# A spectral and gated kernel on one core: eight token tiles instead of six by the seven-product scheme in the first chunk, and GpSimd's stores as operations of the scheduler

## The chip, the cores and the metric

The kernel runs on one core of a Trainium2 chip. The metric is device time in microseconds (us) of one execution; lower is better. Matrix products run on TensorE (PE in the profile, its weight loads PEld), elementwise work on VectorE (DVE) and ScalarE (ACT); GpSimd (POOL) only issues DMA stores and SyncE (SP) only DMA loads. A matmul reads a 128x128 and a 128x512 operand from the on-chip memory and adds up in one of eight PSUM banks.

## The reference

For a sequence of 2048 tokens of 512 features in fp32, it computes the sum of the input, a Fourier mixing and a gated feed-forward of the layer-normed input:

```python
xn = _layernorm(x, axis=-1)
return x + _A_ref(xn, ...) + _B_ref(xn, ...)
# _A_ref: a = xn @ Wre.T; b = xn @ Wim.T      (hidden DFT, 512 x 512)
#         y = Cre @ a - Cim @ b               (sequence DFT, 2048 x 2048)
# _B_ref: h = gelu(xn @ w_gate) * (xn @ w_up); out = h @ w_down   (512 -> 1792 -> 512)
```

## The kernel before

**The products.** Every fp32 operand is split into a high part (rounded, by ScalarE: `split_hi`, L240) and a low part (operand minus high part, by VectorE: `split_lo`, L243). `mm3` (L254) makes a product from three matmuls (high with high, low with high, high with low), all recorded at L257. So a panel loaded from memory passes ScalarE, then VectorE, then TensorE. In the profile `psh`/`psl` and `z311h`/`z311l` are such pairs of parts.

**The sequence DFT** is made in four chunks of 512 output columns, c = 0 to 3. Its token tiles are taken in pairs (k, k+8). A pair's part of a chunk is a 2 by 2 block product. It is made in one of two ways:

- *plain* (only in chunk 0): two panels for each tile and four blocks of columns, 24 matmuls a tile, results in the `z` banks;
- by *seven products* (a Strassen-Winograd form): sums of the DFT blocks and of the tokens are made on VectorE, and seven products are taken in two steps (p = 0: r = 0, 5, 6, 4 with 24 matmuls; p = 1: r = 1, 3, 2 with 18), 42 a pair, in the `m` banks. Step p = 0 loads three panels, makes three sums (`sum_step`, L614) and parks the third, t2, in memory with a GpSimd store; step p = 1 loads t2 again. At the end of a chunk's p = 0 steps ScalarE and VectorE empty the banks (`after`, L1421: the rows L1426 to L1436), and the p = 1 products use the same banks again.

`J` (L31) lists the pairs that go by seven products in chunk 0. From c = 1 on all eight pairs do.

**The hidden DFT.** From the results of chunk 0 and 1, the products y with numbers r = 0, 1 (after chunk 0) and r = 4, 2, 6, 5, 3 (after chunk 1) are made, each in two halves g of 12 matmuls. Their operands z are split like all others (`z400h` is r = 4, g = 0, first half, high part). Each y is copied by ScalarE into two `part` buffers (L542), which GpSimd stores to `partial` in memory: r = 0, 5, 6 plainly (L544 is that store's line, L546 the other's), r = 1, 2, 3, 4 adding to what stands there. One call, `y_out` (L539), makes copies and stores.

**What sets the order.** All operations of the chunks 0 and 1 and of the y products after them, with the first loads and splits of chunk 2, are handed to a list scheduler, `Plan` (L34), and from chunk 2 on the order is written by hand. An operation is added (`add`) with its engine, its cost in us, what must come before it, buffers that it makes and uses, a due time, and mb, the size of its DMA. `deadlines` (L66) works due times back from TensorE's order; an operation that empties a bank gets the end of its product plus 4 unless it is given one. `choose` (L104) takes the earliest that can begin, with more urgent ones preferred; `run` (L142) keeps the clocks. Buffers are 109 of one size (128x512), of which the plan uses 107; a buffer is free again when its last user has ended, and the engine that takes it next then waits for that user, for example for a store's landing. Of DMAs the plan knows a transfer time of 2.6 us per MB, and, for SP's loads only, that no more than eight may be in flight. GpSimd's stores stood inside other operations: the stores of y within the copies on ScalarE, the park of t2 within the third sum on VectorE, a store of `xd` within a subtraction; the plan's own operations on GpSimd's queue for these did nothing (`lambda: None`). The copies of the five last y sums carry a fixed due time:

```python
        plan.add(("yo", r), "a", 1.04, lambda r=r: y_out(0, r), after=[("y", r, 1), *OUT.get(r, ())], makes={("po", r): 2}, holds=both,
                 due=END + 54.4)
        plan.add(("yd", r), "g", 1.2, lambda: None, after=[("yo", r)], uses=[("po", r)], mb=2 * MB)
```

END is the plan's time for the end of chunk 1's products.

Of the kernel before, what the change touches and what calls it, by code (L numbers as in the profile page):

```python
# [11 lines left out]
AF = mybir.ActivationFunctionType  # L12
OP = mybir.AluOpType

P = 128
S = 2048
# [13 lines left out]
SLOTS = 109  # L30
J = (5, 6, 7)  # L31
NP = NF
# [3 lines left out]
class Plan:  # L36
# [15 lines left out]

    def add(self, name, engine, cost, fn, after=(), makes=(), uses=(), due=None, mb=0, banks=(), holds=()):
# [5 lines left out]
        self.ops[name] = dict(e=engine, cost=cost, fn=fn, after=after, makes=dict(makes), due=due, mb=mb, banks=tuple(banks), drains=bool(holds) and engine != "p")  # L59
        self.size.update(makes)  # L60
        for k in (*dict(makes), *uses):
            self.users.setdefault(k, set()).add(name)
        for k in (*banks, *holds):
            self.held.setdefault(k, set()).add(name)

    def deadlines(self):  # L66
# [27 lines left out]
        for n in order:  # L94
# [47 lines left out]
    def run(self):  # L142
# [25 lines left out]
        while any(ready.values()):  # L168
# [39 lines left out]
def fnet_geglu_kernel(ctx: ExitStack, tc: tile.TileContext, x, xt, cs, dh, wgu, wd, out):  # L208
# [299 lines left out]

    yps, zraw, zt = {}, {}, {}

# [12 lines left out]

    def sub_xd(sp, j):
        nc.vector.tensor_sub(xd[sp, j, 0], xd[sp, j, 0], xd[sp, j, 1])
        nc.gpsimd.dma_start(partial[sp, 2, j], xd[sp, j, 0])

    def y_block(r, g, b, js=range(2), first=True):
# [4 lines left out]
        for part in (slice(2), slice(2, 3)):  # L533
            for e in range(2):
                for j in js:
                    mm3(yps[r, j], [u[:, e] for u in dop[r, g]], cols(j), b[e], first and e == 0, not first and e == 1,
                        part=part, late=1)

    def y_out(sp, r, js=range(2)):  # L539
        for j in js:  # L540
            t = slot("part")
            nc.scalar.activation(t, yps[r, j], AF.Copy)  # L542
            if r in (0, 5, 6):
                nc.gpsimd.dma_start(partial[sp, r, j], t)  # L544
            else:
                nc.gpsimd.dma_start(partial[sp, r, j], t, accum_op=OP.add)  # L546

# [65 lines left out]

    def sum_step(i):  # L614

# [618 lines left out]
    plan.dma, land = 12.8, 8.75  # L1234
    plan.flying["s"] = [4.4, 5.7, 7., 8.1]
    for t in range(2, X_AHEAD):
        plan.done(("x", XO[t]), land)
        plan.flying["s"].append(land)
        land += .675
    for i in range(3, LOAD_AHEAD):  # L1240
        plan.done(("pan", i), land)
        plan.flying["s"].append(land)
        land += .675
# [144 lines left out]
    def step_ops(i, late=None):  # L1388
# [3 lines left out]
        def s(j):  # L1392
            if not box:
                box.extend(sum_step(i))
# [180 lines left out]
    for r, g in ((0, 0), (0, 1), (1, 0), (1, 1)):  # L1575
# [3 lines left out]
        if g:  # L1579
            plan.add(("yo", r), "a", 1.04, lambda r=r: y_out(0, r), after=[("y", r, g), *([("res", 0, 0)] if r else ["st2"])],  # L1580
                     makes={("po", r): 2}, holds=[("y", r, j) for j in range(2)])
            plan.add(("yd", r), "g", 1.2, lambda: None, after=[("yo", r)], uses=[("po", r)], mb=2 * MB)
        if (r, g) == (0, 0):
# [14 lines left out]
    for j in range(2):  # L1598
        plan.add(("xd", j), "s", .9, lambda j=j: load_xd(0, j), makes={("xd", j): 2}, mb=2 * MB)
        plan.add(("xds", j), "v", V5, lambda j=j: sub_xd(0, j), after=[("xd", j)], uses=[("xd", j)], due=END - 12)  # L1600
        plan.add(("xdp", j), "g", .01, lambda: None, after=[("xds", j)], uses=[("xd", j)], mb=MB, due=END - 8)
    for kb in range(2):
# [6 lines left out]
    for r in (4, 2, 6, 5, 3):  # L1609
        both = [("y", 1, r, j) for j in range(2)]  # L1610
        for g in range(2):
            plan.add(("y", r, g), "p", 12 * MM, lambda r=r, g=g: z_y(r, g), uses=[("do", r, g)] + [("z", (r, g, e)) for e in range(2)],
                     after=[("dlo", r, g), *(("zlo", (r, g, e)) for e in range(2))], banks=both * (g == 0), holds=both)
        plan.add(("yo", r), "a", 1.04, lambda r=r: y_out(0, r), after=[("y", r, 1), *OUT.get(r, ())], makes={("po", r): 2}, holds=both,
                 due=END + 54.4)
        plan.add(("yd", r), "g", 1.2, lambda: None, after=[("yo", r)], uses=[("po", r)], mb=2 * MB)
    END += 10 * 12 * MM
# [131 lines left out]
```

## Time and profile before

| | |
|---|---|
| time, three runs | 804.59 us median (804.32 to 807.07) |
| the profiled execution | 804.45 us, with a span of 802.4 us |
| TensorE | 794.4 us busy, 3493 instructions, clock granted in full |
| VectorE | 718.8 us busy, 1330 instructions |
| ScalarE | 504.9 us busy, 950 instructions |
| GpSimd | 156.4 us busy, 227 instructions |

The profile is of one execution. A busy TensorE says little alone, since matmuls overlap: what counts is their pitch, the time between the starts of two. Engines wait for each other by semaphores, and the trace names for each wait the engine or DMA that ended it, by inference. Chunk 0 takes the span up to about 90 us, chunk 1 from about 100 to 176 us, the y products between and behind them up to 205 us; the gated part begins near 390 us.

### The profile page before, as it was taken

Reading aid. Unit: us, or ns where it says so; the run is one execution under the profiler, and the core shown is the slowest. Engines: PE = TensorE matmul, PEld = TensorE weight load, DVE = VectorE, ACT = ScalarE, POOL = GpSimd, SP = SyncE. Lnnn points to the kernel's source line nnn. Section 1 sums busy time; section 2 is a strip of 40 time slices with the busy share of each in tenths; the row PEclk is TensorE's granted clock in tenths of the full one; section 3 lists DMA queues with packets and bytes.
Section 4 is the critical chain, followed back from the end, with each engine's and each line's share of the span. In section 5 each row is a group of like instructions: output and inputs, shape, how many; then the busy total and the mean of one; then the engine's idle time right before and its main releaser. Section 6 shows DMA issues by size and latency. Waiting matters only on the chain.

```text
span 802.4 us, 11459 instructions
## 1 busy us (share of the span) xinstructions
PE 794.4 (99%) x3493; PEld 654.4 (82%) x3493; DVE 718.8 (90%) x1330; ACT 504.9 (63%) x950; POOL 156.4 (19%) x227
## 2 busy tenths in 40 slices
PE   9999999999899999999999999999999999999998
PEld 6888888888688888888888888888888888888886
DVE  7999999969899979899999998898778779989787
ACT  6786566547444465364758776766766677576564
POOL 0001410034211131000203423321221233121100
PEclk9999999999999999999999999999999999999999
DMA  9737797868999988778825987868965799887842
GB/s 333 283 119 259 268 353 256 281 230 233 349 351 315 350 289 296 256 272 268 203 79 128 218 161 172 189 109 217 255 126 96 128 232 153 174 211 137 250 105 105
DMA packets 90110, 176.69 MB, mean 220 GB/s; under 512 B 10784, under 2 KB 14400, under 8 KB 89856
## 3 DMA queue, kind: packets, MB, share of 16 engines
q1 hardware_dynamic: 65040, 117.75, 43.7%
q0 software_dynamic: 24720, 57.95, 33.7%
q8 instruction: 27, 0.44, 0.2%
q14 instruction: 35, 0.29, 0.1%
q10 hardware_dynamic: 288, 0.26, 0.1%
HBM read 113.77 MB, written 65.29 MB: 223 GB/s over the span
## 4 chain that ended last, share of the span: by engine, by line
PE 97%; DMA 1%; DVE 1%; ACT 0%; issue 0%; SPq 0%; DVEq 0%; ACTq 0%
PE m L257 31%; PE dn L257 17%; PE b L257 14%; PE c L257 10%; PE a L257 9%; PE y L257 8%; PE z L257 7%; DMA pan<-in_cs 1%; PE warm L1191 1%; DVE psl L246 0%; ACT part L542 0%; DVE dl L246 0%; DVE zr L1514 0%; DVE z410l L246 0%; ACT dh L241 0%
## 5 line engine op out<-in xcount | busy, mean ns | idle before, releaser
L241 ACT ACTIVATE psh<-pan 128x512 fp32r<-128x512 f32 x189 | 108.7, 626 | 82.1 <-DVE pan L628 30.0
L246 DVE TENSOR_TENSOR psl<-pan,psh 128x512 fp32r<-128x512 f32 x189 | 121.3, 682 | 6.0 <-ACT psh L241 5.3
L907 POOL DMA_DIRECT2D partial<-part x94 | 80.9, 870 | 234.0 <-ACT part L906 200.7
L257 PE MATMUL m<-psl,xch 128*128 128x512 f32 x216 | 84.2, 390 | 0.1
L257 PE MATMUL m<-psh,xch 128*128 128x512 f32 x216 | 84.1, 390 | 0.0
L257 PE MATMUL m<-psh,xcl 128*128 128x512 f32 x216 | 84.1, 389 | 0.0
L906 ACT ACTIVATE part<-dn 128x512 f32<-128x512 f32 x94 | 55.4, 604 | 24.2 <-PE dn L257 22.4
L246 DVE TENSOR_TENSOR wl<-ws,wh 128x512 fp32r<-128x512 f32 x84 | 55.1, 684 | 0.1
L241 ACT ACTIVATE wh<-ws 128x512 fp32r<-128x512 f32 x84 | 49.7, 629 | 0.1
L257 PEld LDWEIGHTS m<-psl,xch 128*128 128x128 f32 x216 | 40.6, 188 | 9.1 <-DVE psl L246 0.6
L257 PEld LDWEIGHTS m<-psh,xch 128*128 128x128 f32 x216 | 40.6, 188 | 8.3
L257 PEld LDWEIGHTS m<-psh,xcl 128*128 128x128 f32 x216 | 40.6, 188 | 8.3
L1131 ACT ACTIVATE w<-b 128x512 f32<-128x512 f32 x28 | 16.7, 598 | 47.1 <-PE b L257 47.0
L624 POOL DMA_DIRECT2D t_park<-pan x27 | 15.1, 558 | 140.3 <-DVE pan L624 90.6
L1134 DVE TENSOR_TENSOR w<-c,w 128x512 f32<-128x512 f32 x28 | 19.3, 689 | 24.6 <-ACT w L1131 24.6
L246 DVE TENSOR_TENSOR htl<-s,hth 128x512 fp32r<-128x512 f32 x56 | 36.0, 686 | 4.5 <-ACT hth L241 4.4
L879 DVE TENSOR_TENSOR s<-s 128x512 f32<-128x512 f32 x56 | 37.4, 688 | 1.0
L257 PE MATMUL m<-psh,xa 128*128 128x512 f32 x108 | 37.7, 389 | 0.0
L623 DVE TENSOR_TENSOR pan<-pan 128x512 f32<-128x512 f32 x54 | 35.3, 678 | 0.0
L246 DVE TENSOR_TENSOR wl<-wx,wh 128x512 fp32r<-128x512 f32 x28 | 19.2, 686 | 16.3 <-ACT wh L241 16.3
L241 ACT ACTIVATE hth<-s 128x512 fp32r<-128x512 f32 x56 | 32.4, 642 | 1.0 <-DVE s L879 1.0
L241 ACT ACTIVATE hh<-s 128x512 fp32r<-128x512 f32 x42 | 26.7, 635 | 9.8 <-DVE s L866 7.3
(779 smaller groups left out, 2379.2 us busy)
## 6 DMA issues: line engine op xcount, KB each, us to landing
pan<-in_cs SPq DMA_DIRECT2D x155, 256.0 KB, 5.4
partial<-part POOLq DMA_DIRECT2D x122, 256.0 KB, 5.1
wx<-in_wgu SPq DMA_DIRECT2D x56, 256.0 KB, 4.9
wd<-in_wd SPq DMA_DIRECT2D x28, 256.0 KB, 4.3
acc<-partial SPq DMA_DIRECT2D x28, 256.0 KB, 5.6
t_park<-pan POOLq DMA_DIRECT2D x27, 256.0 KB, 4.8
pan<-t_park SPq DMA_DIRECT2D x27, 256.0 KB, 4.4
zr<-z_park SPq DMA_DIRECT2D x16, 256.0 KB, 4.9
```

The lines of the kernel that those rows point to most:

```text
L241: nc.scalar.activation(t[0], src, AF.Copy, scale=float(sign))
L246: engine.tensor_sub(t[1], src, hi)
L257: nc.tensor.matmul(ps, a[u][:, sl], b[v], start=first and r == 0, stop=last and r == 2, skip_group_check=resumed)
L623: return [lambda: nc.vector.tensor_sub(t3, b22, b12), lambda: nc.vector.tensor_sub(t1, b12, b11), lambda: (nc.vector.tensor_sub(b22, b22, ...
L624: lambda: (nc.vector.tensor_sub(b22, b22, t1), nc.gpsimd.dma_start(t2_park[c, k], b22))]
L879: nc.vector.tensor_sub(t, u, v)
L906: nc.scalar.activation(t, ps[j], AF.Copy)
L907: nc.gpsimd.dma_start(partial[sp, r, j], t, accum_op=OP.add)
L1131: nc.scalar.activation(w, b, AF.Copy)
L1134: nc.vector.tensor_add(w, c, w)
L1191: nc.tensor.matmul(ps, warm[:, :P], warm, start=i == 0, stop=False)
```

## The change

Four edits. `J` gets a fourth pair: chunk 0 has eight plain tiles instead of ten, and four pairs by seven products. GpSimd's stores of y, of t2 and of xd become operations of the scheduler on GpSimd's queue; t2's load then comes after the park's operation instead of after the sum. The scheduler counts transfers in flight on both queues (SP eight, GpSimd seven, an accumulating store as two) and takes an accumulating transfer as 3.3 times as long. The copies of the last five y sums lose their fixed due time.

```diff
-J = (5, 6, 7)
+J = (4, 5, 6, 7)
...
+    def parts(self, o):
+        return round(o["mb"] / .262) * (2 if o["adds"] else 1)
...
                 if e == "s":
-                    at = max([at, o["due"] - self.ahead] + self.flying[e][-8:][:1] * (len(self.flying[e]) > 7))
+                    at = max(at, o["due"] - self.ahead)
+                if o["mb"]:
+                    k, room = self.parts(o), 8 if e == "s" else 7
+                    for when, u in reversed(self.flying[e]):
+                        k += u
+                        if k > room:
+                            at = max(at, when)
+                            break
...
-                self.dma = max(self.dma, at + o["cost"] + 1.1) + o["mb"] * 2.6
+                self.dma = max(self.dma, at + o["cost"] + 1.1) + o["mb"] * 2.6 * (3.3 if o["adds"] else 1)
                 end = self.dma + self.LAND
-                self.flying[e].append(end)
+                self.flying[e].append((end, self.parts(o)))
...
+    def y_copy(r, js=range(2)):
+        for j in js:
+            ypart[r, j] = slot("part")
+            nc.scalar.activation(ypart[r, j], yps[r, j], AF.Copy)
+
+    def y_send(sp, r, js=range(2)):
+        for j in js:
+            nc.gpsimd.dma_start(partial[sp, r, j], ypart.pop((r, j)), **({} if r in (0, 5, 6) else {"accum_op": OP.add}))
...
-                    lambda: (nc.vector.tensor_sub(b22, b22, t1), nc.gpsimd.dma_start(t2_park[c, k], b22))]
+                    lambda: (nc.vector.tensor_sub(b22, b22, t1), park or nc.gpsimd.dma_start(t2_park[c, k], b22))]
...
-                     after=[("S", i - (HS - FIRST[c]), 2)] if key == "t2" else [])
+                     after=[("park", i - (HS - FIRST[c]))] if key == "t2" else [])
...
-            plan.add(("park", i), "g", .01, lambda: None, after=[("S", i, 2)], mb=MB, uses=[("r", i, b22)])
+            plan.add(("park", i), "g", .6, lambda: nc.gpsimd.dma_start(t2_park[c, k], pan_src[i][5]), after=[("S", i, 2)], mb=MB, uses=[("r", i, b22)])
...
-        plan.add(("yo", r), "a", 1.04, lambda r=r: y_out(0, r), after=[("y", r, 1), *OUT.get(r, ())], makes={("po", r): 2}, holds=both,
-                 due=END + 54.4)
-        plan.add(("yd", r), "g", 1.2, lambda: None, after=[("yo", r)], uses=[("po", r)], mb=2 * MB)
+        plan.add(("yo", r), "a", 1.04, lambda r=r: y_copy(r), after=[("y", r, 1), *OUT.get(r, ())], makes={("po", r): 2}, holds=both)
+        plan.add(("yd", r), "g", 1.2, lambda r=r: y_send(0, r), after=[("yo", r)], uses=[("po", r)], mb=2 * MB, adds=r in (1, 2, 3, 4))
```

The copies and sends of r = 0 and 1 and the stores of xd are changed in the same way. The changed kernel's line numbers are 10 to 16 higher (the products L267, high splits L251, low splits L256). It has 3474 matmuls of the products' helper in place of 3480. From chunk 2 on, every engine's order is the same in both kernels.

Three places show what the scheduler makes of it. First ScalarE after chunk 1, where the y products begin: `part` rows are copies of y sums, the first two those of r = 4 and the next two of r = 2; `dh` are high parts of the hidden DFT matrix, `z600h` and the like high parts of z. Before:

```order
L241 ACTIVATE z600h_2197<-zt_2119 128x512
L241 ACTIVATE z601h_2206<-zt_2201 128x512
L241 ACTIVATE dh_2211<-ds_2174 128x512
L241 ACTIVATE dh_2227<-ds_2209 128x512
L241 ACTIVATE dh_2232<-d_2074 128x512
L542 ACTIVATE part_2235<-y_2132 128x512
L542 ACTIVATE part_2238<-y_2133 128x512
L241 ACTIVATE z610h_2244<-zt_2230 128x512
```

And now:

```order
L251 ACTIVATE z600h_2213<-zt_2133 128x512
L553 ACTIVATE part_2216<-y_2146 128x512
L553 ACTIVATE part_2218<-y_2147 128x512
L251 ACTIVATE z601h_2224<-zt_2211 128x512
L251 ACTIVATE dh_2230<-ds_2227 128x512
L251 ACTIVATE dh_2249<-ds_2188 128x512
L251 ACTIVATE dh_2252<-d_2089 128x512
L251 ACTIVATE z610h_2257<-zt_2247 128x512
```

The copies of r = 4 stood behind z601h and three matrix splits and now stand directly behind z600h. Second ScalarE some fifteen rows later, at the end of the y products, with the semaphores that each row waits for (DMASW: a GpSimd transfer, DMAHW: an SP load). Before, the last z splits, the copies of r = 5 and the first panels of chunk 2 (`psh`):

```order
L241 ACTIVATE z301h_2347<-zr_2081 128x512 [waits DMASW5_49,DVE_49,Activation_49]
L241 ACTIVATE z310h_2363<-zr_2091 128x512 [waits DMASW7_49,DVE_49,Activation_49]
L241 ACTIVATE z311h_2377<-zr_2093 128x512 [waits DVE_49]
L542 ACTIVATE part_2401<-y_2314 128x512 [waits DMASW4_49,DMAHW0_49,DMASW2_49,PE_49]
L542 ACTIVATE part_2404<-y_2315 128x512 [waits PE_49,Activation_49]
L241 ACTIVATE psh_2412<-pan_2296 128x512 [waits DMAHW4_49]
L241 ACTIVATE psh_2415<-pan_2408 128x512 [waits DMASW1_49,DVE_49]
```

And now:

```order
L553 ACTIVATE part_2394<-y_2327 128x512 [waits PE_49,Activation_49]
L553 ACTIVATE part_2396<-y_2328 128x512 [waits DMASW3_49,PE_49]
L251 ACTIVATE psh_2408<-pan_2094 128x512 [waits DMAHW2_49,Activation_49]
L251 ACTIVATE psh_2411<-pan_2400 128x512 [waits DMASW4_49,DVE_49,Activation_49]
L251 ACTIVATE z310h_2420<-zr_2322 128x512 [waits DVE_49]
L251 ACTIVATE z311h_2423<-zr_2324 128x512 [waits DMASW5_49,DVE_49,Activation_49]
L251 ACTIVATE psh_2429<-pan_2401 128x512
```

Two panel splits and the copies now stand ahead of z310h and z311h, and psh_2411 and z311h take the buffers of the two r = 2 copies (the transfers DMASW4 and DMASW5 there); before, the buffer of the second r = 2 copy went to VectorE's row z311l. Third VectorE at the end of chunk 1's p = 0 steps, where the banks m are emptied (`c22` and `m4` are the last four of these adds; `pan` is a sum of panels and `psl` a panel's low part). Before:

```order
L1434 TENSOR_TENSOR c22_1794<-m4_1361,u2_1776 128x512
L1434 TENSOR_TENSOR c22_1800<-m4_1369,u2_1786 128x512
L1436 TENSOR_TENSOR m4_1361<-m4_1361,p0_1747 128x512
L1436 TENSOR_TENSOR m4_1369<-m4_1369,p0_1753 128x512
L246 TENSOR_TENSOR psl_1741<-pan_1533,psh_1740 128x512
```

And now:

```order
L1450 TENSOR_TENSOR c22_1785<-m4_1346,u2_1770 128x512
L644 TENSOR_TENSOR pan_1482<-pan_1466,pan_1482 128x512
L1450 TENSOR_TENSOR c22_1799<-m4_1353,u2_1777 128x512
L256 TENSOR_TENSOR psl_1758<-pan_1426,psh_1757 128x512
L1452 TENSOR_TENSOR m4_1346<-m4_1346,p0_1741 128x512
L1452 TENSOR_TENSOR m4_1353<-m4_1353,p0_1749 128x512
```

A panel sum and a low split now stand between the adds. Counted from the start, the first of these m4 adds is VectorE's 305th row before and its 304th now; at the same place of chunk 0 it is the 187th before and the 177th now.

More of the change, by code (lines that the diff above doesn't have):

```diff
@@ L51, in done, with add @@
         self.ends[name] = at
-    def add(self, name, engine, cost, fn, after=(), makes=(), uses=(), due=None, mb=0, banks=(), holds=()):
+    def add(self, name, engine, cost, fn, after=(), makes=(), uses=(), due=None, mb=0, banks=(), holds=(), adds=False):
         after = list(after)
@@ L58, in add @@
             self.products = name
-        self.ops[name] = dict(e=engine, cost=cost, fn=fn, after=after, makes=dict(makes), due=due, mb=mb, banks=tuple(banks), drains=bool(holds) and engine != "p")
+        self.ops[name] = dict(e=engine, cost=cost, fn=fn, after=after, makes=dict(makes), due=due, mb=mb, adds=adds, banks=tuple(banks), drains=bool(holds) and engine != "p")
         self.size.update(makes)
@@ L522, in load_xd, with sub_xd @@
             nc.sync.dma_start(xd[sp, j, h], xt[sp, 1, 2 * h + j])
-    def sub_xd(sp, j):
+    def sub_xd(sp, j, park=False):
         nc.vector.tensor_sub(xd[sp, j, 0], xd[sp, j, 0], xd[sp, j, 1])
-        nc.gpsimd.dma_start(partial[sp, 2, j], xd[sp, j, 0])
+        if not park:
+            nc.gpsimd.dma_start(partial[sp, 2, j], xd[sp, j, 0])
     def y_block(r, g, b, js=range(2), first=True):
@@ L537, in y_block @@
                         part=part, late=1)
+    def y_copy(r, js=range(2)):
[5 more added lines that the diff above has]
+            nc.gpsimd.dma_start(partial[sp, r, j], ypart.pop((r, j)), **({} if r in (0, 5, 6) else {"accum_op": OP.add}))
     def y_out(sp, r, js=range(2)):
         for j in js:
[L541 to L546, printed above, removed]
+            y_copy(r, [j])
+            y_send(sp, r, [j])
     def fetch_z(sp, kb, g):
@@ L1234, in fnet_geglu_kernel @@
     plan.dma, land = 12.8, 8.75
-    plan.flying["s"] = [4.4, 5.7, 7., 8.1]
+    plan.flying["s"] = [(t, 1) for t in (4.4, 5.7, 7., 8.1)]
     for t in range(2, X_AHEAD):
         plan.done(("x", XO[t]), land)
-        plan.flying["s"].append(land)
+        plan.flying["s"].append((land, 1))
         land += .675
@@ L1241, in fnet_geglu_kernel @@
         plan.done(("pan", i), land)
-        plan.flying["s"].append(land)
+        plan.flying["s"].append((land, 1))
         land += .675
@@ L1599, in fnet_geglu_kernel @@
         plan.add(("xd", j), "s", .9, lambda j=j: load_xd(0, j), makes={("xd", j): 2}, mb=2 * MB)
-        plan.add(("xds", j), "v", V5, lambda j=j: sub_xd(0, j), after=[("xd", j)], uses=[("xd", j)], due=END - 12)
-        plan.add(("xdp", j), "g", .01, lambda: None, after=[("xds", j)], uses=[("xd", j)], mb=MB, due=END - 8)
+        plan.add(("xds", j), "v", V5, lambda j=j: sub_xd(0, j, True), after=[("xd", j)], uses=[("xd", j)], due=END - 12)
+        plan.add(("xdp", j), "g", .6, lambda j=j: nc.gpsimd.dma_start(partial[0, 2, j], xd[0, j, 0]), after=[("xds", j)], uses=[("xd", j)], mb=MB, due=END - 8)
     for kb in range(2):
```

10 lines of the change are left out of this document (5 added, 5 removed).

## Prediction

> **What bounds the kernel now.** I read the page first, then the chain of waits by stretches, then the timelines of the one stretch where TensorE stands still. The page:
>
> ```profile
> span 802.4 us, 11459 instructions
> PE 794.4 (99%) x3493; PEld 654.4 (82%) x3493; DVE 718.8 (90%) x1330; ACT 504.9 (63%) x950; POOL 156.4 (19%) x227
> PE 97%; DMA 1%; DVE 1%; ACT 0%; issue 0%; SPq 0%; DVEq 0%; ACTq 0%
> ```
>
> The chain is TensorE for 97% of the span, so time can be saved only by fewer products or by closing TensorE's gaps. The chain from the start to 110 us, then from 170 to 300 us (start, length, what):
>
> ```profile
> 60.69 28.56 PE m L257 x126
> ...
> 179.52 18.88 PE y L257 x82
> 199.72 7.84 DMA pan<-in_cs
> 207.56 1.28 DVE psl L246 x2
> 208.88 74.88 PE m L257 x329
> ```
>
> 28.56/126 gives a product's pitch: 0.2267 us. Between long runs at this pitch one hole is left in this part, at 199 to 209 us, the end of the second chunk. TensorE's timeline there (start, busy, instruction; in brackets its wait):
>
> ```profile
> 202.99 0.61 PE L257 MATMUL y<-z310l,dh 128*128 128x512 f32 x2
> 204.54 0.73 PE L257 MATMUL y<-z311l,dh 128*128 128x512 f32 x2 [0.94 <-DVE z311l L246]
> 205.12 0.39 PE L257 MATMUL m<-psh,xa 128*128 128x512 f32 x1
> 207.08 0.50 PE L257 MATMUL m<-psl,xa 128*128 128x512 f32 x1 [1.57 <-DVE psl L246]
> ...
> 208.88 0.50 PE L257 MATMUL m<-psl,xch 128*128 128x512 f32 x1
> 209.22 0.40 PE L257 MATMUL m<-psh,xcl 128*128 128x512 f32 x1
> ```
>
> Five products are left out. From 202.99 to 209.22 us twelve products start (two, two, one, one, the five, one), worth 12 x 0.2267 = 2.72 us; 6.23 us went by. **The hole is 3.51 us.** VectorE's timeline says whose fault it is:
>
> ```profile
> 198.20 0.69 DVE L246 TENSOR_TENSOR z310l<-zr,z310h 128x512 fp32r<-128x512 f32 x1
> 203.80 0.69 DVE L246 TENSOR_TENSOR z311l<-zr,z311h 128x512 fp32r<-128x512 f32 x1 [4.91 <-DMA partial<-part]
> ...
> 206.34 2.49 DVE L246 TENSOR_TENSOR psl<-pan,psh 128x512 fp32r<-128x512 f32 x4
> ```
>
> VectorE stands for 4.91 us on one row, z311l, until a GpSimd store has landed: z311l takes the buffer of the second copy of the y sum r=2. All rows behind it, the sums and low splits (psl) of the third chunk's first panels, come late by as much. The second wait of TensorE, on psl, is the tail of the same wait. (2.49-0.69)/3 = 0.60 us is VectorE's pitch for a 128x512 row.
>
> Why that store landed so late, from ScalarE's copies and GpSimd's issues:
>
> ```profile
> 186.20 1.06 ACT L542 ACTIVATE part<-y 128x512 f32<-128x512 f32 x2
> 188.72 1.08 ACT L542 ACTIVATE part<-y 128x512 f32<-128x512 f32 x2
> ```
> ```profile
> 187.21 1.81 POOL L546 DMA_DIRECT2D partial<-part  x2 [3.00 <-ACT part L542]
> 188.41 1.18 POOL L410 DMA_DIRECT2D d_park<-dh  x1
> 189.01 1.12 POOL L410 DMA_DIRECT2D d_park<-dl  x1
> 194.03 0.89 POOL L546 DMA_DIRECT2D partial<-part  x1 [3.90 <-ACT part L542]
> 196.74 0.87 POOL L546 DMA_DIRECT2D partial<-part  x1 [1.81 <-ACT z310h L241]
> ```
>
> The r=2 copies were done by 189.80, but the stores went out at 194.03 and 196.74. The releasers named had long been done, so it was something else: two accumulating stores of r=4 (187.21) and two parks were still under way. I read it as a queue that takes about seven transfers, an accumulating one counting as two; that is my reading of the issue times, not a row. Landing times of the stores of y from 186 to 198 us, then of the parks from 178 to 186 us, when little else was moving:
>
> ```profile
> DMA to landing us min/median/max: 5.2/6.7/8.6
> DMA to landing us min/median/max: 2.3/2.4/2.4
> ```
>
> **The change, part by part.**
>
> *One more seven-product pair.* 10 plain tiles of 24 products become 8, and 3 pairs of 42 become 4: 240+126 = 366 products become 192+168 = 360. Six fewer on the chain: 6 x 0.2267 = **-1.36 us**, sure as long as TensorE stays fed.
>
> What it costs is on VectorE. For the pair, eleven rows (seven low splits, four sums) replace four low splits: +7 x 0.60 = 4.2 us. One half-width split goes (-0.3), and four half-width sums and two splits of x move from the second chunk to the first (about 2.5 us; I take half a row for half the width). VectorE has no slack to take this in:
>
> ```profile
> 145.00:165.00 20.00, 20.00 (x90) 16.58 (x89) 19.84 (x34) 9.90 (x19) 2.34 (x5) 1.00 0.72 243
> 165.00:175.00 10.00, 10.00 (x46) 8.29 (x45) 3.55 (x6) 2.38 (x6) 4.15 (x8) 1.00 0.99 343
> ```
>
> (columns: length, PE, PEld, DVE, ACT, POOL, clock, DMA, GB/s.) It is busy throughout until 165 us and first idles in the next 10 us. So the question is only how far ahead of TensorE it stands where the banks are drained. The adds that release the m4 banks, and TensorE's first use of the next panel:
>
> ```profile
> 77.73 1.28 DVE L1436 TENSOR_TENSOR m<-m,p 128x512 f32<-128x512 f32 x2
> 144.71 1.28 DVE L1436 TENSOR_TENSOR m<-m,p 128x512 f32<-128x512 f32 x2
> ```
> ```profile
> 79.57 0.39 PE L257 MATMUL m<-psh,xch 128*128 128x512 f32 x1
> 146.36 0.39 PE L257 MATMUL m<-psh,xch 128*128 128x512 f32 x1
> ```
>
> The first of the two adds ends about 0.68 us after its start, so the leads are 79.57-78.41 = 1.16 us and 146.36-145.39 = 0.97 us. At the first drain the new order puts these adds ten VectorE rows earlier (6.0 us), and the products come 24 earlier (5.44 us): a lead of 1.16+6.00-5.44 = 1.7 us, more than before. The scheduler puts rows without haste behind them. At the second drain the adds stand one row earlier (0.6 us) and the products six (1.36 us): 0.97+0.60-1.36 = 0.2 us. It just holds; a row more would show. I put 0.1 us there, with 0 and 0.6 (one row) as ends.
>
> *Stores as own operations, counted in flight.* No instruction is added on the path: the copies and sends are the same, only placed by the scheduler. The t2 load now waits for the issue of the park and not for the sum alone; those loads stand far ahead of their use, and I price it at nothing. If that cover were gone, a park's landing (2.4 to 8.6 us by the rows above) would show.
>
> *The r copies lose the fixed deadline* (END+54.4), and get the one from their banks. This is what moves the late store. In before, r=4 and r=2 end on TensorE at these rows, the second 24 products after the first:
>
> ```profile
> 181.68 0.61 PE L257 MATMUL y<-z411l,dh 128*128 128x512 f32 x2
> 187.12 0.61 PE L257 MATMUL y<-z211l,dh 128*128 128x512 f32 x2
> ```
>
> The r=4 sums were ready at 182.3 and copied only at 186.20, behind five splits. Now the copies stand right behind z600h (the order shows it), so they run at about 181 to 182.5, some 4 us earlier, and their stores go out near 183. They land by 5.2 to 8.6 us, at 188 to 191.5; the r=2 stores then go out at about 188 to 190.5 and 191 to 193.5 instead of 194.03 and 196.74. With the median 6.7 us the second lands at 198 to 200, against 203.7 before.
>
> What is due next there: its buffer is now taken by z311h, one step earlier in the chain than z311l. The first z311h product stands four before the 202.99 row, at 202.08, and 1.36 us earlier now: 200.72. The split takes 0.63 us, so the landing must come by about 200.0. My interval ends just there. A landing at the late end costs 0 to 0.3 us, and every us beyond it a us of TensorE. With the store in time, VectorE goes on to the third chunk's panels with no hole, and **the 3.51 us go**; for small leads in the rows behind (the first psl comes within 0.1 us of its use by my count) and for this landing I add 0.3 us, with 0 and 1.5 as ends.
>
> From the third chunk on all engines' orders are the same as before, so nothing is added.
>
> **Sum.** The profiled execution took 804.45 us, 2.05 around its span of 802.4, and stands 0.14 below the median 804.59. 804.45-1.36-3.51+0.10+0.30 = 799.98, **about 800.0 us**.
>
> **Rivals.**
>
> *A: the store still lands late.* For it speaks the traffic there:
>
> ```profile
> 185.00:195.00 10.00, 10.00 (x46) 8.29 (x45) 10.00 (x18) 8.05 (x16) 3.81 (x5) 1.00 0.95 253
> ```
> ```profile
> 185.09 14.54 SPq L1382 DMA_DIRECT2D pan<-in_cs  x12
> ```
>
> The DMA engines are 95% busy and SP issues twelve loads in that stretch, so a 256 KB accumulating store takes 5.2 to 8.6 us and not 2.4; the new plan also fetches two z tiles and two panels late. If the second r=2 store keeps its place against TensorE (203.7-1.36 = 202.35), z311h ends at 203.0 in place of 200.72: a wait of 2.3 us of the 3.51 stays. 804.45-1.36-3.51+2.3+0.1 = 802.0 us; with the whole hole back, 803.1. Against it: the r=4 copies move ahead by 4 us. The Trainium skill, DMA: Bandwidth & Descriptors, section Queues, rings and completion order, says that each DMA engine takes turns between the queues that have work, a packet at a time. By that rule the store shares its engines with SP's loads however early GpSimd issues it, and the trace agrees (5.2 us at least under load, 2.4 without). Priced by the rows, the slow landing (8.6 in place of 6.7) is 1.9 us later at the middle of my interval, 200.9: a wait of 0.9 us, 800.9 us in all.
>
> *B, the slower one: VectorE becomes the bound at the first chunk's drain.* If the 4.2+2.5-0.3 = 6.4 us of rows stand ahead of the m4 adds, the lead of 1.16 us turns into a wait of 5.2 us, and with the late store's hole in place too the time is 804.45+5.2-1.36 = 808.3 us; with one more row late at the second drain 808.9. It decides where the lead at the first drain is under zero. For it: VectorE is 90% busy and 100% here. The Trainium skill, Perfetto Trace Analysis, section Identifying the Most-Contended Engine, judges Vector by its busy share and Tensor by weight loads, not by matmul time. By that rule Vector (90%) is more contended than Tensor (82%), and work added to it would lengthen the span, to about 808; the chain here, 97% TensorE, does not agree. Against B: the new order has the adds ten rows earlier.
>
> *C: the change does not do what it says.* The order shows the six products gone and the copies moved, so I give it no chance of its own.
>
> **How the numbers follow.** Forecast (the hole closes, or nearly): 0.60. A: 0.30. B: 0.08. Unnamed, to either side: 0.02. A measurement of this kernel can tell a change of about 0.5% from none; that is 4.02 us, so the bounds are 800.57 and 808.61. The forecast with its ends runs from 799.2 (neither added wait, and 0.4 us for what my rows resolve) to 801.7 (a wait of 1.5 us at the landing, 0.6 at the second drain); of its 0.60 I put 0.52 below 800.57, and half of the unnamed, so faster is 0.53. Of B and the unnamed about 0.05 lies above 808.61. Within 0.5% is the rest: 0.42. The range must leave out 0.2 at most: from 799.2, through the forecast and all of A, to 803.2; B is left out.
>
> **What would show it.** Right: 3474 in place of 3480 products at the helper's line; z311h and z311l without a DMA wait, no wait of TensorE over 0.5 us between 195 and 210 us; the r=4 copies near 182 us and the r=2 stores out before 194; the second drain's psh product following its neighbour within 0.3 us. A is right if a row of ScalarE or VectorE at about 200 us again waits for `partial<-part`. B is right if TensorE waits for an m add near 74 or 145 us. My forecast is wrong in mechanism if TensorE waits at a place where no row above stands, such as the first chunk's plain tiles, or if a load queued behind GpSimd's parks comes late.

## Result: 0.8% faster, a little more than the range allowed

The changed kernel takes **798.94 us** (median of 4 runs, 798.84 to 799.29) against 805.46 us (4 runs, 804.32 to 807.07) before it: a ratio of 0.9921, with a 95% interval of 0.9902 to 0.9939. A second time, beside other runs, it took 799.11 us against 804.52 us: 0.9926 (0.9909 to 0.9943). The forecast was 800.0 us, with a range from 799.2 to 803.2.

The page of the profiled execution (799.29 us) says little by itself; VectorE even works a little more:

```profile
span 797.2 us, 11453 instructions
PE 792.6 (99%) x3487; PEld 652.9 (82%) x3487; DVE 722.3 (91%) x1336; ACT 505.7 (63%) x952; POOL 157.2 (20%) x228
```

What moved is the end of the second chunk. ScalarE's copies of y r=4 and then r=2, GpSimd's stores of them, and z311h, which now takes the buffer of the second r=2 copy:

```profile
181.90 1.06 ACT L553 ACTIVATE part<-y 128x512 f32<-128x512 f32 x2
...
186.49 1.09 ACT L553 ACTIVATE part<-y 128x512 f32<-128x512 f32 x2
...
199.97 0.63 ACT L251 ACTIVATE z311h<-zr 128x512 fp32r<-128x512 f32 x1
```
```profile
183.64 1.79 POOL L557 DMA_DIRECT2D partial<-part  x2
...
188.71 0.91 POOL L557 DMA_DIRECT2D partial<-part  x1 [1.54 <-ACT z500h L251]
192.24 0.86 POOL L557 DMA_DIRECT2D partial<-part  x1 [2.61 <-ACT z511h L251]
```

The r=4 copies run 4.3 us earlier than before, the r=2 stores go out at 188.71 and 192.24 in place of 194.03 and 196.74, the second of them has landed at 198.88 in place of 203.71, and z311h waits for no DMA. TensorE at the same place:

```profile
199.66 0.61 PE L267 MATMUL y<-z301l,dh 128*128 128x512 f32 x2
200.13 0.50 PE L267 MATMUL y<-z310h,dh 128*128 128x512 f32 x1
200.46 0.39 PE L267 MATMUL y<-z310h,dl 128*128 128x512 f32 x1
...
202.53 0.61 PE L267 MATMUL y<-z311l,dh 128*128 128x512 f32 x2
202.99 0.39 PE L267 MATMUL m<-psh,xa 128*128 128x512 f32 x1
```

Where 3.51 us were lost, 0.12 us are (200.46-199.66 less three products of 0.2267). The second drain costs as little:

```profile
144.86 0.39 PE L267 MATMUL m<-psh,xf12l 128*128 128x512 f32 x1
145.12 0.50 PE L267 MATMUL m<-psh,xch 128*128 128x512 f32 x1
145.46 0.40 PE L267 MATMUL m<-psl,xch 128*128 128x512 f32 x1
```

0.60 us for two products is 0.15 us over the pitch.

### The profile page after: what moved, and what is told of

The parts are those of the page before. It is cut to its first block, busy times and chain, and to the rows that moved or that the text cites. A ratio compares the mean times of both kernels' runs of the same rounds, so it can differ in the third digit from the quotient of the medians.

```text
span 797.2 us, 11453 instructions
## 1 busy us (share of the span) xinstructions
PE 792.6 (99%) x3487; PEld 652.9 (82%) x3487; DVE 722.3 (91%) x1336; ACT 505.7 (63%) x952; POOL 157.2 (20%) x228
## 4 chain that ended last, share of the span: by engine, by line
PE 99%; DVE 0%; issue 0%; ACT 0%; DVEq 0%
PE m L267 33%; PE dn L267 17%; PE b L267 14%; PE c L267 10%; PE a L267 10%; PE y L267 9%; PE z L267 6%; PE warm L1207 1%; DVE dl L256 0%; DVE z411l L256 0%; ACT dh L251 0%; DVE ds L433 0%; DVE p L1002 0%; PE warm L1209 0%; DVE warm L1203 0%
## 5 line engine op out<-in xcount | busy, mean ns | idle before, releaser
L251 ACT ACTIVATE psh<-pan 128x512 fp32r<-128x512 f32 x196 | 112.3, 625 | 74.6 <-DVE pan L644 29.6
L256 DVE TENSOR_TENSOR psl<-pan,psh 128x512 fp32r<-128x512 f32 x196 | 125.9, 681 | 5.4 <-ACT psh L251 4.7
L923 POOL DMA_DIRECT2D partial<-part x94 | 81.0, 868 | 234.9 <-ACT part L922 200.9
L267 PE MATMUL m<-psh,xch 128*128 128x512 f32 x224 | 87.3, 390 | 0.0
L267 PE MATMUL m<-psl,xch 128*128 128x512 f32 x224 | 87.2, 389 | 0.0
L267 PE MATMUL m<-psh,xcl 128*128 128x512 f32 x224 | 87.2, 389 | 0.0
L256 DVE TENSOR_TENSOR wl<-ws,wh 128x512 fp32r<-128x512 f32 x84 | 55.0, 683 | 0.3 <-ACT wh L251 0.2
L251 ACT ACTIVATE wh<-ws 128x512 fp32r<-128x512 f32 x84 | 49.6, 629 | 0.8 <-DMA xT_hl<-xT51h 0.7
L267 PEld LDWEIGHTS m<-psh,xch 128*128 128x128 f32 x224 | 42.0, 188 | 9.1 <-DVE m L1452 0.3
L267 PEld LDWEIGHTS m<-psh,xcl 128*128 128x128 f32 x224 | 42.0, 188 | 8.7
L267 PEld LDWEIGHTS m<-psl,xch 128*128 128x128 f32 x224 | 42.1, 188 | 8.7
L557 POOL DMA_DIRECT2D partial<-part x28 | 20.8, 787 | 106.3 <-ACT part L553 97.5
L256 DVE TENSOR_TENSOR htl<-s,hth 128x512 fp32r<-128x512 f32 x56 | 35.9, 684 | 4.2 <-ACT hth L251 4.1
L267 PE MATMUL m<-psh,xa 128*128 128x512 f32 x112 | 39.0, 389 | 0.0
L256 DVE TENSOR_TENSOR wl<-wx,wh 128x512 fp32r<-128x512 f32 x28 | 19.2, 686 | 16.2 <-ACT wh L251 16.2
L251 ACT ACTIVATE hth<-s 128x512 fp32r<-128x512 f32 x56 | 32.4, 642 | 1.0 <-DVE s L895 1.0
L267 PE MATMUL dn<-hl,wh 128*128 128x512 f32 x84 | 32.8, 390 | 0.0
```

What stands on the lines that cost most here:

```text
L251: nc.scalar.activation(t[0], src, AF.Copy, scale=float(sign))
L256: engine.tensor_sub(t[1], src, hi)
L267: nc.tensor.matmul(ps, a[u][:, sl], b[v], start=first and r == 0, stop=last and r == 2, skip_group_check=resumed)
L557: nc.gpsimd.dma_start(partial[sp, r, j], ypart.pop((r, j)), **({} if r in (0, 5, 6) else {"accum_op": OP.add}))
```

## The experiments

Every kernel was compared with the kernel before on the same chip; the kernel before had medians of 804.67 us beside the first four, 804.52 beside the next four and 805.30 beside the last three.

**1. The kernel before once more.** No edit.

> The kernel before, unchanged, to see what of its time repeats. In the profiled execution 3.96 us lay between the last matmul and the end of the span, against 3.28 us after the change, though the last instructions are the same. Theory 1: the 0.68 us are chance of the last store, so here the tail may be anything from 3.2 to 4.0 us and the hole at the end of the second chunk stays at 3 to 4.5 us. Rival: the tail belongs to the kernel, and is 3.9 to 4.0 us again. If the hole itself varies from run to run by the store's landing, the times spread over 804.3 to 807 us again.

804.43 us (12 runs, 802.23 to 806.71), ratio 0.9992 (0.9978 to 1.0005). The profiled execution took 806.62 us, 2.17 us more than the one the prediction was made from. VectorE's wait, and TensorE behind it:

```profile
204.86 0.69 DVE L246 TENSOR_TENSOR z311l<-zr,z311h 128x512 fp32r<-128x512 f32 x1 [5.86 <-DMA partial<-part]
```
```profile
203.11 0.61 PE L257 MATMUL y<-z310l,dh 128*128 128x512 f32 x2
205.61 0.73 PE L257 MATMUL y<-z311l,dh 128*128 128x512 f32 x2 [1.88 <-DVE z311l L246]
206.18 0.39 PE L257 MATMUL m<-psh,xa 128*128 128x512 f32 x1
208.14 0.72 PE L257 MATMUL m<-psl,xa 128*128 128x512 f32 x1 [1.57 <-DVE psl L246]
208.66 1.05 PE L257 MATMUL m<-psh,xa 128*128 128x512 f32 x2
209.52 0.63 PE L257 MATMUL m<-psl,xa 128*128 128x512 f32 x1
...
211.65 0.41 PE L257 MATMUL m<-psh,xch 128*128 128x512 f32 x1
```

The same wait is 5.86 in place of 4.91 us, so the hole's size differs from one execution to the next. And here something is added: from 208.66 to 211.65 us seven products start, 0.427 us apart and not 0.227. That is 1.4 us more, after two waits that cost 2.0 and 1.7 us. The granted clock falls in this stretch (columns: length, PE, PEld, DVE, ACT, POOL, granted clock, DMA share, GB/s); in the execution profiled for the prediction it is 1.00 there:

```profile
208.50:212.00 3.50, 3.50 (x10) 2.68 (x10) 3.50 (x7) 2.04 (x5) 1.05 (x2) 0.55 1.05 414
```

The Trainium skill, TensorE: Matmul & The Clock Gate, section Part 1: The HAM clock gate (the "warmup" mystery), says that the array falls to half its clock after an idle window of some 3.4 us, and gives 426.7 ns from one product to the next at half clock. The trace agrees on the half clock, with 427 ns, and not on the idle time as one piece: no wait here is longer than 2.0 us. The last store landed in 2.3 us, as before (2.4).

**2. The due time alone.** In the kernel before:

```diff
-        plan.add(("yo", r), ..., holds=both, due=END + 54.4)
+        plan.add(("yo", r), ..., holds=both)
```

> Only the fixed due time of the five last y copies is taken away from the kernel before. Theory 1 (the deadline moves the late store): the r=4 copies run near 183 us, the r=2 stores go out before 194 us, no row at 199 to 206 us waits more than 0.5 us for a store, and the time is 804.5-3.4 = 801.1 us, 3.4 us under before. Rival (the counting of transfers in flight is what does it): the hole stays at 2 us or more and the time is 802.5 to 804.6 us.

801.17 us, ratio 0.9952 (0.9938 to 0.9966). The gain is as Theory 1 has it, and the r=4 copies stand at 182.11 us. But its account of the waits is wrong: rows still wait for these stores, and longer than 0.5 us.

```profile
ACT part L542 <- DMA partial<-part: 4.0, 1, 4.0
...
DVE z310l L246 <- DMA partial<-part: 2.1, 1, 2.1
```

TensorE fell only 1.2 us behind its pitch between 203 and 207 us, because the waiting rows were hardly due yet.

**3. The fourth pair alone.** In the kernel before: `J = (4, 5, 6, 7)`.

> Only the fourth seven-product pair, with the old stores, old counting and the old due time. Six products fewer give 1.36 us. Theory 1: the r=4 copies stay late (near 187 us), the second r=2 store lands near 202 us and a panel split of the third chunk waits for it, so 1 to 3 us of the hole stay: 800.7 to 802.7 us. Rival B of the prediction (VectorE bounds the first chunk once the pair is there): a wait of 1 us or more at one of the drains (near 74 or 145 us), 803 us or more.

800.37 us, ratio 0.9943 (0.9929 to 0.9957), just below Theory 1's range. Its reason fails more clearly. The r=4 copies are late as before the change, a panel split waits long for a store of r=2, and TensorE loses nothing there:

```profile
202.65 3.24 ACT L241 ACTIVATE psh<-pan 128x512 fp32r<-128x512 f32 x6 [4.95 <-DMA partial<-part]
```

The store landed at 202.58 us, against 203.71 before with six products more ahead of it. So a landing that is as late, counted by TensorE's work, costs 3.5 us in one kernel and nothing in the other. **Theory 2** was formed here: what counts is which row takes the buffer, when that row is due, and what stands behind it on its engine. This run has also something of rival B. ScalarE waited for a load, VectorE for ScalarE, and the second drain came late:

```profile
59.40 0.63 ACT L241 ACTIVATE dh<-d 128x512 fp32r<-128x512 f32 x1 [2.06 <-DMA d<-in_dh]
```
```profile
62.00 0.43 DVE L1348 TENSOR_TENSOR xs<-x,x 128x256 f32<-128x256 f32 x1 [1.51 <-ACT x L1288]
```
```profile
144.86 0.39 PE L257 MATMUL m<-psh,xf12l 128*128 128x512 f32 x1
145.78 0.50 PE L257 MATMUL m<-psh,xch 128*128 128x512 f32 x1 [0.53 <-DVE m L1436]
```

A product starts 0.92 us after its neighbour: 0.69 us lost (0.80 with the product behind it), where the changed kernel, with its stores placed by the scheduler, loses 0.15 in all. From 62 to 146 us VectorE is busy without a break in this run, so it can't make up what it lost at 62 us; that this wait is what the drain lost is argued from that and was not run by itself.

**4. The stores alone.** The changed kernel with `J = (5, 6, 7)`.

> The changed kernel with three pairs as before: stores as own operations, counted, and no fixed due time. Theory 1: the hole closes as in the changed kernel, so 3.4 us under before, about 801.1 us, and 1.4 us over the changed kernel with four pairs. Rival (the two parts need each other, the hole closes only by the order that the fourth pair brings): 803 us or more.

800.55 us, ratio 0.9946 (0.993 to 0.9962): the hole closes without the fourth pair, too, with no wait of TensorE between 180 and 215 us. The second r=2 store landed at 201.47 us only, but in this kernel the r=2 buffers go to SP loads that are not urgent.

**5. The changed kernel once more.** No edit.

> The changed kernel, unchanged. In six profiled executions so far the last store of 128 KB landed in 1.71 to 1.75 us in three and in 2.34 to 2.38 us in three, with the same instructions around it. Theory 1: this is chance of the execution, so here it is either, and the median stays at 798.9 us. Rival: the landing belongs to the kernel, 1.7 us again here. The second r=2 store lands near 198.9 us again and the hole stays closed (under 0.3 us in all between 199 and 207 us).

799.11 us (798.76 to 799.42), and the hole stays closed. The last store landed in 1.7 us again. In the thirteen profiled executions of this study none lay between the two levels.

**6. The due time put back** into the changed kernel.

> The changed kernel with the fixed due time of the last five y copies put back. Theory 1 as predicted (the missing due time is what closes the hole): the copies of r=4 run near 187 us, the r=2 stores land after 202 us, and 2 us or more of the hole come back: 801 to 802.5 us. Theory 2, formed after the run with only the pair (there the r=2 store landed at 202.58 as late as before, a panel split waited 4.9 us for it, and TensorE lost nothing): what counts is which row takes the copy's buffer. Here a sum and a split of the third chunk's next step take the r=2 buffers, rows that are not due yet, so the hole stays closed: 798.9 to 799.6 us.

798.77 us, ratio 0.9922 (0.9903 to 0.994): no slower than the changed kernel, as Theory 2 says. The copies of r=4 and r=2 run together at 185.90 us, the store's landing is waited for on ScalarE, and the waiting row is a split that is not due:

```profile
185.90 2.04 ACT L553 ACTIVATE part<-y 128x512 f32<-128x512 f32 x4
...
203.30 1.15 ACT L251 ACTIVATE psh<-pan 128x512 fp32r<-128x512 f32 x2 [2.11 <-DMA partial<-part]
```

What the due time does cost is small and elsewhere: a late copy holds its PSUM banks, and the product of r=6 wants them.

```profile
185.75 0.61 PE L267 MATMUL y<-z211l,dh 128*128 128x512 f32 x2
186.53 0.50 PE L267 MATMUL y<-z600h,dh 128*128 128x512 f32 x1 [0.17 <-ACT part L553]
```

0.78 us for two products: 0.33 us lost.

**7. Without the counting.** In the changed kernel GpSimd's limit becomes 99 (with accumulating stores counted once) and the factor 3.3 goes. The edit does a third thing: a transfer now counts once whatever its size, on both queues, so SP's loads of two blocks count as one, as in the kernel before:

```diff
-                    k, room = self.parts(o), 8 if e == "s" else 7
+                    k, room = 1, 8 if e == "s" else 99
...
-                        k += u
+                        k += 1
...
-                ... + o["mb"] * 2.6 * (3.3 if o["adds"] else 1)
+                ... + o["mb"] * 2.6
```

> The changed kernel, with GpSimd's transfers no longer limited to seven in the plan, accumulating stores counted once and priced as plain ones; stores stay own operations, no due time. Theory 2: z310l takes the first r=2 copy's buffer (landing near 196 to 199 us, wanted by 200.6) and a y copy the second: at most 0.5 us of the hole, 798.9 to 799.6 us. Rival (the counting is what places the stores well): 800.5 us or more.

**798.09 us** (797.94 to 798.36), ratio 0.9913 (0.9895 to 0.9932), lower than every theory had it and lower than all six runs of the changed kernel beside it (798.76 at least). It is the fastest kernel of this study. The three parts of the edit were not run apart, so which of them brings the gain is open. Its chain from 160 to 300 us has no wait:

```profile
159.97 14.96 PE m L267 x66
174.93 27.20 PE y L267 x120
202.13 76.21 PE m L267 x336
```

The chain of short operations at the start of the y products, which costs the changed kernel and the one before 0.4 us near 178 us, is gone as well: the sum `ds` of the hidden DFT's matrix stands directly ahead of z410l on VectorE, and no longer behind z411l. The scheduler gives that place already when only SP's loads are counted once, and not when only the factor 3.3 is taken away.

**8. Plain in place of accumulating stores,** in the kernel before:

```diff
-            if r in (0, 5, 6):
+            if r in (0, 5, 6) or sp == 0 and r in (4, 2):
```

> The kernel before with the r=4 and r=2 y stores plain instead of accumulating (so these two products replace what stands in memory instead of being added to it); the order of every engine and every buffer is the same. If GpSimd's queue holds about seven transfers and an accumulating one counts as two, the r=2 stores go out right after the copies, near 190 us instead of 194 and 197, and land near 197 to 199 us; z311l does not wait, the hole closes: 801.0 us, 3.5 us under before. Rival (the stores are held back by the traffic on the DMA engines, not by their kind): they go out near 194 and 197 us again and the time is 804 us or more.

800.46 us, ratio 0.9943 (0.9926 to 0.996). With every order and buffer the same, the r=2 stores go out right behind the copies:

```profile
187.06 1.16 POOL L544 DMA_DIRECT2D partial<-part  x2 [2.98 <-ACT part L542]
...
189.59 1.14 POOL L544 DMA_DIRECT2D partial<-part  x2 [0.24 <-issue]
```

They were 194.03 and 196.74 us as accumulating ones. They landed no sooner after their issue, though (the two r=2 stores of this run):

```profile
DMA to landing us min/median/max: 7.1/7.1/7.1
```

So it is the kind of the stores that held the issue back. As accumulating stores they went out right behind two landings, those of the stores of r=4. In the kernel before (the first line gives the issue of these, the last the shortest, median and longest time to their landing):

```profile
L546 POOL DMA_DIRECT2D partial<-part x2: 912/1042/1172, 187.2 to 187.8; - x2
...
DMA to landing us min/median/max: 6.5/7.5/8.6
```

They landed at 193.73 and 196.43, and the two stores of r=2 went out at 194.03 and 196.74, 0.3 us after each. In the changed kernel it is the same: landings at 188.41 and 191.93, issues at 188.71 and 192.24. This bears out the reading of a queue with a limit, as far as it goes; how many places it has was not measured by itself.

**9. One buffer fewer.** In the kernel before `SLOTS = 108`, with the plan's own number of 107 kept. Every engine's order is that of before; only the buffers change hands.

> The kernel before with 108 buffers in place of 109; the plan and every engine's order are the same, only which buffer a row takes differs. The second r=2 copy's buffer now goes to ScalarE's copy of the second half of y r=5 (wanted from 198.4 us on), with two panel splits of the third chunk behind it on ScalarE, and not to z311l. Theory 2 (the taker and what stands behind it set the loss, not the landing alone): z311l does not wait; the copy waits until 203.7 us, the panel splits end at 205.3 and the low part at 205.9, where TensorE wants it at 204.1, so about 1.8 us of the 3.5 stay: 802.5 to 803 us. Rival (the late landing costs what it costs, whoever takes the buffer): 804 us or more.

802.64 us, ratio 0.9979 (0.9963 to 0.9995). The second r=2 store goes out at 196.37 and lands at 203.84 us, within 0.4 us of before, but a copy on ScalarE takes its buffer, with panel splits behind it:

```profile
203.94 0.60 ACT L542 ACTIVATE part<-y 128x512 f32<-128x512 f32 x1 [4.93 <-PE y L257]
204.44 2.18 ACT L241 ACTIVATE psh<-pan 128x512 fp32r<-128x512 f32 x4
```

The releaser named, PE, had long been done; the r=2 store landed just before. TensorE's wait is now on the panel split, and with all that follows from it 2.3 us. Other buffers change hands too. The first r=2 copy's goes to z310l, which now waits for that store, and is still in time for its product at 202.92:

```profile
201.98 0.69 DVE L246 TENSOR_TENSOR z310l<-zr,z310h 128x512 fp32r<-128x512 f32 x1 [3.80 <-DMA partial<-part]
```

So one number changed, no order changed and the landing stayed, and the loss went from 3.5 to 2.3 us.

**10. A fifth pair.** The changed kernel with `J = (3, 4, 5, 6, 7)`, and token operands taken one by one.

> The changed kernel with a fifth seven-product pair (six more products saved, 1.36 us), and the pair's token operands taken only as they come to be. It asks how near VectorE is to being the bound, rival B of the prediction. VectorE's add that frees the m4 bank stands twelve rows later at the first drain (some 5 to 7 us, as some are of half width) and TensorE's use 24 products earlier (5.4 us); the lead in the changed kernel was 0.9 us. Theory (VectorE is the bound from the fifth pair on): TensorE waits 8 to 12 us at the first drain, near 70 us, and the time is 803 to 809 us. Rival (VectorE has room left and the scheduler finds it): 797.5 to 798 us.

805.88 us, ratio 1.0017 (1.0004 to 1.003). Six products fewer and 6.8 us slower than the changed kernel. VectorE is busy throughout and TensorE is not (columns: length, PE, PEld, DVE, ...), and at the first drain the m4 add stands directly before the product:

```profile
50.00:80.00 30.00, 25.11 (x95) 16.48 (x94) 29.51 (x65) 20.80 (x38) 1.08 (x2) 1.00 0.42 136
```
```profile
76.23 1.30 DVE L1454 TENSOR_TENSOR m<-m,p 128x512 f32<-128x512 f32 x2
```
```profile
76.98 0.50 PE L267 MATMUL m<-psh,xch 128*128 128x512 f32 x1 [1.41 <-DVE m L1454]
```

The time is in the range that the expectation gave, and TensorE loses some 9 us, but all along from 54 to 77 us and not at the drain alone, as the expectation had it. The row waited for longest is one of ScalarE's:

```profile
PE m L267 <- ACT xa L251: 2.1, 2, 1.6
```

ScalarE itself waits for rows of VectorE in this stretch, and VectorE is the engine that is hardly ever idle, so rival B's mechanism is real; with this scheduler its point lies between four pairs and five.

**11. No counting, and the due time back.**

> The changed kernel without the counting of GpSimd's transfers (as in the run of 798.09 us) and with the fixed due time back. The r=2 buffers go to a load of SP and to a panel sum of the third chunk's first steps on VectorE. Theory 2: the second r=2 store lands near 203 us as with the due time before, the panel sum waits for it, and 1 to 3 us of TensorE's hole come back, as the sum is due at once: 799 to 801 us. Rival (due time and counting do not matter once the stores are own operations): 798.0 to 798.4 us.

799.15 us, ratio 0.9937 (0.9918 to 0.9955). This lies at the low end of Theory 2's range, and not for its reason: the second r=2 store landed at 199.92 us, in time, and nothing of the hole came back. What it lost against run 7 is mostly the wait for PSUM banks of run 6, larger here:

```profile
185.62 0.39 PE L267 MATMUL y<-z211l,dh 128*128 128x512 f32 x1
186.42 0.50 PE L267 MATMUL y<-z600h,dh 128*128 128x512 f32 x1 [0.41 <-ACT part L553]
```

0.80 us for one product: 0.57 us lost.

## Why the prediction was right, and where it was wrong

**Right: what bounds the kernel, and the hole.** The six products went. The hole of 3.51 us closed to 0.12. The r=2 stores went out within the intervals that were given (188 to 190.5, 191 to 193.5), the second landed at 198.88 (198 to 200 was given), and z311h began at 199.97, close to the latest start that the prediction allowed it (200.72-0.63 = 200.1).

**Right in kind: VectorE's leads.** The first drain had a lead and the second next to none. The lead at the first was forecast at 1.7 us; the first add and the product, in the changed kernel:

```profile
72.64 1.28 DVE L1452 TENSOR_TENSOR m<-m,p 128x512 f32<-128x512 f32 x2
```
```profile
74.21 0.39 PE L267 MATMUL m<-psh,xch 128*128 128x512 f32 x1
```

72.64+0.68 = 73.32 is the end of the first add, and 74.21-73.32 = 0.89 us. The adds came 5.09 us earlier (72.64 in place of 77.73) and not 6.00: ten rows at 0.60 us each were too much. It cost nothing. At the second, 0.15 us were lost where 0.10 were allowed.

**Wrong: the low end of the range.** The step that failed is "799.2 (neither added wait, and 0.4 us for what my rows resolve)". The median came 0.26 us lower. The sum was mis-sized in three places:

- the allowance of 0.30 us for the landing: 0.12 came;
- the end of the span, which had no term. The last store is one of SyncE's, which issues stores of the result too. It goes out 0.49 us after the last matmul in both kernels, and landed in 2.4 us before and in 1.7 us after (the landing of SP's last store, of before and of after):

```profile
DMA to landing us min/median/max: 2.4/2.4/2.4
```
```profile
DMA to landing us min/median/max: 1.7/1.7/1.7
```

- the step from a profiled execution to a median: the profiled execution of the change was 0.35 us above its median.

799.98-0.18-0.68-0.35+0.05 (second drain) = 798.82, which leaves 0.12 us of 798.94 unexplained. Against before the gain is larger still (5.4 to 6.5 us in place of 4.6), since the sum took the hole of one execution, 3.51 us, for the hole. Run 1 shows an execution with a larger one and a stretch at half clock behind it, and the kernel before spreads over 802 to 807 us in these runs while the changed kernel stays within 0.7 us. The mean granted clock of each execution goes with that spread. Of the 63 executions of the kernel before in the experiments, 31 have a mean of 0.998 or less, as run 1's profiled one has, with a median of 806.2 us; the other 32 have a median of 804.0. All ten of the changed kernel have 1.000. So about half of the executions before seem to pay for a stretch like run 1's, and against the others the gain is about 5 us; in a profile the stretch was seen once.

**Too narrow: the cause.** "The r copies lose the fixed deadline ... This is what moves the late store" is true of the kernel in hand, where the r=2 stores follow the landings of r=4, and yet the gain does not hang on it. Run 6 puts the due time back and is as fast; run 3 keeps it, with stores as late, and has no hole; run 9 keeps every order and the landing, and loses less. Run 8 shows the other half: with the same taker, a store that lands at 197.32 in place of 203.71 us closes the hole too. So the hole needed both, a late landing and the row that happened to get the copy's buffer: z311l, the next row that TensorE needed, with the third chunk's panels behind it. Almost any change of order deals the buffers anew, and each of the runs 2, 3, 4, 6, 7 and 11 closed the hole or most of it (in run 2, 1.2 us stayed).

**The rivals.** A (the landing still late) did not come about. The rule of the Trainium skill that went with it (DMA: Bandwidth & Descriptors, Queues, rings and completion order) fits the traces as far as they go: among SP's loads run 8's plain stores of 256 KB took 7.1 us to land, within the 5.2 to 8.6 us of the accumulating ones, where plain ones without much traffic took 2.3 to 2.4. No run shows the taking of turns itself. When a store may be issued is another matter, and there the kind decided. B had a first sign with the pair alone, where the old plan lets VectorE wait 1.51 us, and came in full with the fifth pair. The rule of the Trainium skill that went with B (Perfetto Trace Analysis, Identifying the Most-Contended Engine) would, as the prediction read it, have had the change slower at VectorE's 91% against 82% of weight loads; the time went down, so here that comparison does not decide; the lead at the drains does. The section names a second measure for TensorE, the share of its peak that the matmuls reach, which was not worked out.

**Left open:** why the last store lands in 1.7 or in 2.3 to 2.4 us. It was 2.3 to 2.4 in both executions of the kernel before and in runs 4 and 8, and 1.7 to 1.8 in the other nine: run 9, with the same order as before, and both executions of the changed kernel are among them. Also open is which part of run 7's edit gains. Why a load held ScalarE in run 3 and not in the changed kernel can be read from the two traces: in run 3 it went out at 53.95 us behind three panel loads and landed at 59.38, in the changed kernel at 53.67 behind one and landed at 57.03, before ScalarE's row at 57.83.

## What to carry to other kernels

Where a row waits for a store because it was dealt the store's buffer, ask first who got the buffer and when that row is due; another taker can be worth as much as an earlier store, and one number of the pool can try it. A stall that depends on a landing differs from execution to execution, so take its size from several profiles before it goes into a sum. When work moves to an engine that is busy throughout, count its lead where the other engine drains banks: with 0.9 us left at the first drain a fourth pair was all but free, and a fifth cost 6.8 us.

## What the runs showed of the hardware

An accumulating store of 256 KB ahead in GpSimd's queue delays the issue of the ones behind it more than a plain one: with the order the same, 194.03 and 196.74 us became 189.59 and 190.19. In the kernel before and the changed one the next two accumulating stores went out 0.3 us after the landings of the two ahead. After waits of 2.0 and 1.7 us with three products between them, TensorE took 0.427 us for each of seven products, at a granted clock of 0.55 in that stretch; after waits of 1.1 and 1.7 us it did not. The last store of 128 KB landed in 1.7 to 1.8 or in 2.3 to 2.4 us, and in none of thirteen executions between.
